# State products as 64x64 blocks on the four quarters of the array, in a new issue order

## The chip, the cores and the metric

The program runs on one core of one Trainium2 chip. The metric is the device time of one execution in microseconds. The kernel before takes 740.38 us, the median of 3 runs (739.6 to 740.51). One further execution was recorded by the hardware profiler; the rows below are of that one.

## The reference

The kernel computes three layers one after the other, all in float32 (4 batches, 8 heads, 576 positions, head size 64; 2304 tokens of width 512):

```python
scores = scale * np.matmul(q, k.transpose(0, 1, 3, 2))
gamma = 1.0 - 2.0 ** (-5.0 - np.arange(H))                    # one decay per head
Dmat = np.where(rel >= 0, gamma[:, None, None] ** rel, 0.0)   # rel = query position - key position
x = np.matmul(scores * Dmat, v)                               # retention; heads side by side: 2304 x 512

h = x @ w_in                                                  # 512 -> 1024
e = np.exp(h - h.max(-1)); sm = e / (e.sum(-1) + 1e-09)
solu = h * sm
ln = (solu - solu.mean(-1)) / np.sqrt(solu.var(-1) + 1e-06) * g_ln
x = ln @ w_out                                                # 1024 -> 512

r = np.maximum(x @ w_in2, 0.0)                                # 512 -> 2048
out = (r * r) @ w_out2                                        # 2048 -> 512
```

The weights of both feed-forward layers arrive as 64-bit floats and are taken apart on the chip.

## The kernel before, in words

The 2304 tokens are 18 tiles of 128. The retention is computed tile by tile in linear form: within a tile scores, mask and values; from tile to tile a running state (the sum of k times v for each head, 64x64), which is started anew at each of the 4 batches.

The order of the whole work is written out by hand in the string `ORDER`: one letter is one step, and a letter's n-th appearance is its n-th tile (or weight job). Each engine executes its share of the steps in that order. A number behind a letter below (S14) is that count, from 0. The letters that matter here:

- `q`, `k`, `v`, `l`: loads of queries (256 tokens, two DMAs), keys, values (128 tokens) and of one half-megabyte weight piece (`raw`), all issued by SyncE's queue. Each issue waits until the one eight before it has landed.
- `D`, `d`: decays of q and k (GpSimd; for the first tile VectorE). `T`, `t`: transposes of q (for two tiles) and k on TensorE, copied out by ScalarE.
- `S` (a_sc): scores of a tile, 8 products of 64 rows, into two banks; VectorE multiplies each bank by the mask.
- `K` (a_kv): the state's own products, 8 of 64x64, copied out by ScalarE into `st`, a 128x128 block for each pair of heads, whose two off-diagonal 64x64 blocks stay zero (two memsets at the start).
- `U` (a_state): state times queries, 4 products with that 128x128 block. It has nothing to do at the first tile of a batch. `V` (a_pv): masked scores times values, 8 products, added into the same bank `x`; ScalarE copies the bank to `x2`.
- `f`, `c`, `h`, `o`: decoding of one weight piece: ScalarE, then VectorE (three operations, L152 to L154) and GpSimd (one), then ScalarE (the high part) and VectorE (the rest: L168 for w_in and the last layer, L170 for w_out). Pieces 0 to 7 are w_in, 8 to 15 w_out, 16 to 47 the last layer's.
- `A`, `B` (m1): the two halves of x @ w_in; VectorE takes the maximum. `E`, `N`, `s`, `P`: softmax and norm on ScalarE and VectorE. `Z` (ln_T): transposes, out by ScalarE and VectorE.
- `m` (m2): a 128x256 piece of ln @ w_out, 24 matmuls over all eight w_out pieces. `3`, `4`: the last layer's two products for 384 tokens. At its end each 128 tokens are copied to an output tile `o` (two buffers) and sent by two DMAs.

All products in these layers are three matmuls (high times high, high times rest, rest times high). Score, state and value products are plain float32, which the profile records as two matmuls each.

PSUM has eight banks: five of them (`r_bank`) go round among q and k transposes, scores, `x`, `Z` and `m`, in the order in which they are asked for; two are for `A`, `B` and `3`; one is for the state `st`.

Of the kernel before, what the change touches and what calls it, by code (L numbers as in the profile page):

```python
# [8 lines left out]
F32 = mybir.dt.float32  # L9
# [3 lines left out]
AF = mybir.ActivationFunctionType  # L13
# [8 lines left out]


ORDER = """
UllkxzqyflkqcfvkhcdtkDldDvfvqThdlkctSvKoSTtfhkoUldqVKckvtVUDdXlhoSkKfdcSvdqVlDfKdTvgUtovcvlAltVSSfXK
DkUTthchUooVVkKSftckhUVfqlolhvfdKkcoSdqTAdvBtEUDVKftNXkcvBTSvlKSdqktDUKldsUhEkcVShNtdqDUkoKfvVdPfVlK
hToctdfAoBSXScTlUtVKDScXfcttUUhofkVsVvKSShUPEhkdNZlVKsZdvABETNlostlotUcVfhohPoKXPASBmmENZmvmcsAZPXfU
BEmSVKlNXvmABUsPcXVENmZmlflKsAZBEmNPlAXsZPFfBZElmhcmNlfAslBhXmEcNsmPAlhXZBElPNlmAZsXBlENsomPAmXBlEmP
oNfcZmXAfXBENsPlcosZhmXABhPmZEmoNZAscllllBhElPNmXmsoomAPBElNsPZmAflBhZEmNsWYmcmPomYmmZlZmhommmmQffcc
3h3ho3fc4fo34h4oc34fhc3ol43fc3hfhf44oco3c434fhhoc3o34fcfh3ohl4fcl34foch3olch43of44ho3c4lf3lhcf3oc4fh  # L30
oc3h3f4o4hfoc343fhocl43hco3fhc43oflh4oc3fc43h4oho433fc44h43o344
"""


# [1 line left out]
def tile_retention_solu_relu2(  # L36
# [19 lines left out]
    nc = tc.nc  # L56
# [4 lines left out]
    P = 128  # L61
# [37 lines left out]
    def r_bank(shape, name):  # L99
        return bank("r", shape, name, 5)  # L100
# [2 lines left out]
    kdecay = at.tile([P, NPAT, H], F32, name="kdecay")  # L103
    masks = at.tile([P, 2, 2, P // 2], F32, name="masks")

    sts = [at.tile([P, KD, P], F32, name=f"st{i}") for i in range(2)]
    ident = const.tile([P, P], F32, name="ident")
    gln = const.tile([P, KF], F32, name="gln")
    mhalf = const.tile([P, 1], F32, name="mhalf")
# [3 lines left out]
    def x_cols(o, n):  # L113
        return x2[o // XG][:, :, o % XG:o % XG + n]
# [50 lines left out]
    def job_lo(j):  # L165
# [3 lines left out]
        else:  # L169
            nc.vector.scalar_tensor_tensor(l, t, g, h.bitcast(F32), ALU.mult, ALU.subtract)  # L170

    def wi_jobs(c):
        w = slice(c * JC, (c + 1) * JC)
        for i in range(KD):
            jobs.append((
                lambda r_, i=i: nc.sync.dma_start(
                    out=r_, in_=w_in[i * P:(i + 1) * P, 2 * c * JC:2 * (c + 1) * JC]),
                lambda x, i=i: (wi_h, wi_l)[x][i][:, w], None))

    def wo_jobs(i):  # L180
# [95 lines left out]
    def a_kv(t):  # L276
        pos = t * P % S
        if pos + P == S:
            return
        fresh = pos == 0 or pos + P > S  # L280
        r0 = S - pos if pos + P > S else 0
        if fresh:
            state["s"] = bank("s", [P, KD * D], "st", 1)
        p_ = state["s"]
        for c in range(KD):
            for e in range(2):
                h = 2 * c + e
                nc.tensor.matmul(p_[D * e:D * (e + 1), c * D:(c + 1) * D], ks[t][r0:P, h], vs[t][r0:P, h],
                                 start=(fresh and c == 0), stop=True, skip_group_check=True)
        st[t] = sts[t % 2]  # L290
        for e in range(2):
            r = slice(D * e, D * (e + 1))
            nc.scalar.activation(st[t][r, :, r], p_[r].rearrange("p (c d) -> p c d", c=KD), AF.Copy)

    res = {}

    def a_state(t):
        pos = t * P % S  # L300
        if not pos:
            return
        p_ = res[t] = r_bank([P, KD, P], "x")
        i = slice(0, min(P, S - pos) // 2)
        for c in range(KD):
            nc.tensor.matmul(p_[:, c].rearrange("p (e i) -> p e i", e=2)[:, :, i], st[t - 1][:, c],
                             qT[t][:, c, :, i], start=(c == 0), stop=False, skip_group_check=True)

    def a_pv(t):
        fresh = t not in res  # L310
        p_ = r_bank([P, KD, P], "x") if fresh else res.pop(t)
        for c in range(KD):
            for e in range(2):
                nc.tensor.matmul(p_[D * e:D * (e + 1), c], vs[t][:, 2 * c + e], sm[t][:, e, c],  # L314
                                 start=(fresh and c == 0), stop=True, skip_group_check=True)
        nc.scalar.activation(x_cols(t * P, P), p_, AF.Copy)


    xhl, hb, ee, lnv, lnT = {}, {}, {}, {}, {}
# [121 lines left out]
    def m4(i):  # L441
# [6 lines left out]
        for s in range(SUB):  # L448
            t = slice(s * P, (s + 1) * P)
            nc.tensor.matmul(acc[b][s], gh[:, t], uh[:, 1], start=(c == 0), stop=False)  # L450
            nc.tensor.matmul(acc[b][s], gh[:, t], ul[:, 1], start=False, stop=False)  # L451
            nc.tensor.matmul(acc[b][s], gl[:, t], uh[:, 1], start=False, stop=(c == KF2 - 1))  # L452
            if c == KF2 - 1:
                o = bw["p"].tile([P, DM], F32, tag="o", name="o", bufs=2)
                nc.scalar.activation(o, acc[b][s], AF.Copy)

                rows = out[b * TB + s * P:b * TB + (s + 1) * P, :].rearrange("(i e) d -> e i d", e=2)
                for e in range(2):
                    nc.sync.dma_start(out=rows[e], in_=o[D * e:D * (e + 1)])

    for c in range(FF // JC):
        wi_jobs(c)
# [5 lines left out]
    with tc.manual_schedule():  # L468
        make_identity(nc, ident)
        nc.gpsimd.memset(mhalf, -0.5)  # L470
        for x in sts:
            nc.gpsimd.memset(x, 0.0)

        def causal_masks():

# [24 lines left out]
        def rest_units():  # L500
# [5 lines left out]
            cols = x2[0].rearrange("p k n -> p (k n)")  # L506
            for j, tag in enumerate("ant"):
                free_cols[tag] = [cols[:, JC * n:JC * (n + 1)] for n in (2 * j, 2 * j + 1)]

        steps = {  # L510
            "q": a_load_q, "k": lambda t: a_load(t, k, ks, "k", 4), "v": lambda t: a_load(t, v, vs, "v", 4),
# [68 lines left out]
```

## Time and profile before

| what | value |
|---|---|
| median of 3 runs | 740.38 us (739.6 to 740.51) |
| the profiled execution | 738.71 us, of which the span from first to last instruction 737.0 us |
| TensorE (PE) busy | 704.6 us, 96% |
| VectorE (DVE) busy | 412.1 us, 56% |
| ScalarE (ACT) busy | 325.8 us, 44% |
| GpSimd (POOL) busy | 144.3 us, 20% |
| TensorE's mean granted clock | 0.992 of full speed |

The span has three stretches. Up to about 120 us the retention runs, with all loads of q, k, v and the first weight pieces; here the other engines are busy too. From there to about 327 us the first feed-forward layer dominates, then the last one. Busy shares are means over all three.

### The profile page before, as it was taken

What the parts mean: (1) busy time and instruction counts of PE and PEld (TensorE: products, weight loads), DVE (VectorE), ACT (ScalarE), POOL (GpSimd) and SP (SyncE); (2) the same over time, 40 slices, a digit from 0 to 9 for tenths busy, and PEclk for the clock granted to TensorE, in tenths of its full rate; (3) what the DMA queues carried; (4) which work ended last, traced back from release to release, by engine and by line L of the source; (5) the groups of instructions that cost most, each with busy time, mean ns of one, the idle gap of its engine ahead of it and who ended that gap; (6) DMA issues with size and microseconds to landing.
All of it is one profiled execution on the core that took longest, in us unless ns stands there. A gap on an engine that the chain in (4) does not pass through costs nothing.

```text
span 737.0 us, 11541 instructions
## 1 busy us (share of the span) xinstructions
PE 704.6 (96%) x4560; PEld 639.7 (87%) x4560; DVE 412.1 (56%) x735; ACT 325.8 (44%) x645; POOL 144.3 (20%) x129
## 2 busy tenths in 40 slices
PE   1999979999999999999999999999999999999996
PEld 1888868999899898998999989989999899998995
DVE  4688897665765885638888887222332232232221
ACT  4576855444642653535565554322322332233222
POOL 3675671121211321102323231000000000000000
PEclk9999998999999999999999999999999999999998
DMA  9999980110000010103233320300100010001001
GB/s 186 217 207 252 206 199 1 44 44 29 29 29 1 30 58 1 30 3 113 90 111 97 105 86 1 87 1 0 26 20 1 0 44 1 0 1 44 1 0 44
DMA packets 64358, 44.90 MB, mean 61 GB/s; under 512 B 40368, under 2 KB 57904, under 8 KB 64304
## 3 DMA queue, kind: packets, MB, share of 16 engines
q1 hardware_dynamic: 64304, 44.16, 25.6%
q8 instruction: 36, 0.59, 0.3%
q14 instruction: 18, 0.15, 0.1%
HBM read 39.44 MB, written 4.72 MB: 60 GB/s over the span
## 4 chain that ended last, share of the span: by engine, by line
PE 87%; DVE 5%; DMA 3%; issue 1%; ACT 1%; SPq 1%; POOL 1%; ACTq 0%; DVEq 0%; POOLq 0%
PE acc L452 9%; PE acc L451 9%; PE m L428 9%; PE m L426 9%; PE m L427 9%; PE acc L450 9%; PE m L398 5%; PE m L400 5%; PE m L399 5%; PE h L334 4%; PE h L336 4%; PE h L335 4%; PE lnT L388 2%; DMA raw<-in_moe_w_in_dram 2%; PE sc L272 1%; PE x L314 1%
## 5 line engine op out<-in xcount | busy, mean ns | idle before, releaser
L436 DVE TENSOR_TENSOR g<-rl 128x384 f32<-128x384 f32 x96 | 59.2, 617 | 190.4 <-ACT rl L435 189.9
L435 ACT ACTIVATE rl<-m 128x384 f32<-128x384 f32 x96 | 46.8, 488 | 194.3 <-PE m L428 194.2
L428 PE MATMUL m<-xh,ul 128*128 128x384 f32 x384 | 129.4, 337 | 0.0
L426 PE MATMUL m<-xh,uh 128*128 128x384 f32 x384 | 129.2, 336 | 0.0
L427 PE MATMUL m<-xl,uh 128*128 128x384 f32 x384 | 128.9, 336 | 0.0
L452 PE MATMUL acc<-uh,gl 128*128 128x512 f32 x288 | 113.9, 395 | 0.5 <-DVE gl L438 0.5
L451 PE MATMUL acc<-ul,gh 128*128 128x512 f32 x288 | 113.6, 394 | 0.0
L450 PE MATMUL acc<-uh,gh 128*128 128x512 f32 x288 | 112.0, 389 | 0.0
L398 PE MATMUL m<-lh,woh 128*128 128x256 f32 x288 | 82.0, 285 | 0.0
L400 PE MATMUL m<-lh,wol 128*128 128x256 f32 x288 | 81.5, 283 | 0.0
L399 PE MATMUL m<-ll,woh 128*128 128x256 f32 x288 | 81.3, 282 | 0.0
L426 PEld LDWEIGHTS m<-xh,uh 128*128 128x128 f32 x384 | 72.2, 188 | 3.8
L427 PEld LDWEIGHTS m<-xl,uh 128*128 128x128 f32 x384 | 72.1, 188 | 3.7
L438 DVE TENSOR_TENSOR gl<-g,gh 128x384 fp32r<-128x384 f32 x96 | 63.8, 665 | 17.1 <-ACT gh L437 5.4
L428 PEld LDWEIGHTS m<-xh,ul 128*128 128x128 f32 x384 | 72.0, 188 | 0.0
L452 PEld LDWEIGHTS acc<-uh,gl 128*128 128x128 f32 x288 | 54.0, 187 | 12.4 <-DVE gl L438 1.0
L437 ACT ACTIVATE gh<-rl 128x384 fp32r<-128x384 f32 x96 | 50.5, 526 | 30.4 <-PE acc L451 14.4
L451 PEld LDWEIGHTS acc<-ul,gh 128*128 128x128 f32 x288 | 54.0, 188 | 9.3
L450 PEld LDWEIGHTS acc<-uh,gh 128*128 128x128 f32 x288 | 54.1, 188 | 8.8
L334 PE MATMUL h<-wih,xh 128*128 128x512 f32 x144 | 57.6, 400 | 0.1
L155 POOL TENSOR_TENSOR x<-x 128x512 int32<-128x512 int32 x24 | 35.1, 1463 | 110.8 <-DVE x L154 93.7
L336 PE MATMUL h<-wih,xl 128*128 128x512 f32 x144 | 56.3, 391 | 0.0
(84 smaller groups left out, 1182.3 us busy)
## 6 DMA issues: line engine op xcount, KB each, us to landing
raw<-in_moe_w_in_dram SPq DMA_DIRECT2D x24, 512.0 KB, 3.9
raw<-in_moe_w_out_dram SPq DMA_DIRECT2D x24, 512.0 KB, 3.3
out_dram<-o SPq DMA_DIRECT2D x36, 128.0 KB, 2.4
k<-in_k_dram SPq DMA_DIRECT2D x16, 256.0 KB, 7.8
q<-in_q_dram SPq DMA_DIRECT2D x16, 256.0 KB, 7.2
v<-in_v_dram SPq DMA_DIRECT2D x16, 256.0 KB, 6.5
q<-in_q_dram SPq DMA_DIRECT2D x4, 128.0 KB, 5.9
k<-in_k_dram SPq DMA_DIRECT2D x4, 128.0 KB, 7.3
```

Of the source, the lines that this page charges most:

```text
L334: nc.tensor.matmul(p_, h_[:, i], wi_h[i][:, cols], start=(i == 0), stop=False)
L336: nc.tensor.matmul(p_, l_[:, i], wi_h[i][:, cols], start=False, stop=(i == KD - 1))
L398: nc.tensor.matmul(p_, wo_h[i][:, w], h_[:, i], start=(i == 0), stop=False)
L399: nc.tensor.matmul(p_, wo_h[i][:, w], l_[:, i], start=False, stop=False)
L400: nc.tensor.matmul(p_, wo_l[i][:, w], h_[:, i], start=False, stop=(i == KF - 1))
L426: nc.tensor.matmul(p_, uh[:, 0, w], xh, start=(j == 0), stop=False)
L427: nc.tensor.matmul(p_, uh[:, 0, w], xl, start=False, stop=False)
L428: nc.tensor.matmul(p_, ul[:, 0, w], xh, start=False, stop=(j == KD - 1))
L438: nc.vector.tensor_tensor(gl, g, gh.bitcast(F32), ALU.subtract)
L450: nc.tensor.matmul(acc[b][s], gh[:, t], uh[:, 1], start=(c == 0), stop=False)
L451: nc.tensor.matmul(acc[b][s], gh[:, t], ul[:, 1], start=False, stop=False)
L452: nc.tensor.matmul(acc[b][s], gl[:, t], uh[:, 1], start=False, stop=(c == KF2 - 1))
```

## The change

Four things change.

1. The state `st` holds only the two diagonal 64x64 blocks of a pair of heads: one copy of 128x256 instead of two of 64x256, and no memsets. `U` has 8 products of 64x64 instead of 4 of 128x128. For an odd pair the results go to the other half of the partitions, so that four products in a row lie on the four quarters of the array. Even pairs go to a bank `x0`, odd ones to `x1`; `V` adds to the same two banks, and two copies of 128x256 bring them out instead of one of 128x512.
2. With odd pairs exchanged, the rows of w_in are exchanged to match: such a piece is loaded by two DMAs of 64 rows.
3. `ORDER` is written anew, with the same letters in the same numbers.
4. Output tiles are six columns of the tokens that are done (`x2[0]`) instead of two buffers. The very last one is copied half by VectorE and half by ScalarE, and its two DMAs are issued from two queues.

```diff
 ORDER = """
-UllkxzqyflkqcfvkhcdtkDldDvfvqThdlkctSvKoSTtfhkoUldqVKckvtVUDdXlhoSkKfdcSvdqVlDfKdTvgUtovcvlAltVSSfXK
...
+llxffklyfkczqlcqfcvdlDhdThkcltDUkfovSKvdTthdVcqvSkktoDflUhKVdcvSUKtVodkqTSXktfcdUlvVKtKShShlDvXhUldV
...
 """
-    sts = [at.tile([P, KD, P], F32, name=f"st{i}") for i in range(2)]
+    sts = [at.tile([P, KD, D], F32, name=f"st{i}") for i in range(2)]
...
+    def wi_load(r_, i, c):
+        w = w_in[i * P:(i + 1) * P, 2 * c * JC:2 * (c + 1) * JC]
+        if i % 2 == 0:
+            nc.sync.dma_start(out=r_, in_=w)
+        else:
+            nc.sync.dma_start(out=r_[:D], in_=w[D:])
+            nc.sync.dma_start(out=r_[D:], in_=w[:D])
...
-        for e in range(2):
-            r = slice(D * e, D * (e + 1))
-            nc.scalar.activation(st[t][r, :, r], p_[r].rearrange("p (c d) -> p c d", c=KD), AF.Copy)
+        nc.scalar.activation(st[t], p_.rearrange("p (c d) -> p c d", c=KD), AF.Copy)
...
+    def halves(c, e):
+        return slice(D * e, D * (e + 1)), slice(D * (e ^ c % 2), D * ((e ^ c % 2) + 1))
+
+    def x_banks():
+        return [r_bank([P, KD // 2, P], f"x{j}") for j in range(2)]

     def a_state(t):
...
-        p_ = res[t] = r_bank([P, KD, P], "x")
+        p_ = res[t] = x_banks()
         i = slice(0, min(P, S - pos) // 2)
         for c in range(KD):
-            nc.tensor.matmul(p_[:, c].rearrange("p (e i) -> p e i", e=2)[:, :, i], st[t - 1][:, c],
-                             qT[t][:, c, :, i], start=(c == 0), stop=False, skip_group_check=True)
+            for e in range(2):
+                r, o = halves(c, e)
+                nc.tensor.matmul(p_[c % 2][o, c // 2].rearrange("p (e i) -> p e i", e=2)[:, :, i], st[t - 1][r, c],
+                                 qT[t][r, c, :, i], start=(c < 2), stop=False, skip_group_check=True)

     def a_pv(t):
...
-                nc.tensor.matmul(p_[D * e:D * (e + 1), c], vs[t][:, 2 * c + e], sm[t][:, e, c],
-                                 start=(fresh and c == 0), stop=True, skip_group_check=True)
-        nc.scalar.activation(x_cols(t * P, P), p_, AF.Copy)
+                o = halves(c, e)[1]
+                nc.tensor.matmul(p_[c % 2][o, c // 2], vs[t][:, 2 * c + e], sm[t][:, e, c],
+                                 start=(fresh and c < 2), stop=True, skip_group_check=True)
+        for j in range(2):
+            nc.scalar.activation(x_cols(t * P, P)[:, j::2], p_[j], AF.Copy)
...
-                o = bw["p"].tile([P, DM], F32, tag="o", name="o", bufs=2)
-                nc.scalar.activation(o, acc[b][s], AF.Copy)
+                last = (b, s) == (NBLK - 1, SUB - 1)
+                o = free_cols["o"].pop(0)
+                free_cols["o"].append(o)
+                if last:
+                    hw = DM // 2
+                    nc.vector.tensor_copy(o[:, hw:], acc[b][s][:, hw:])
+                    nc.scalar.activation(o[:, :hw], acc[b][s][:, :hw], AF.Copy)
+                else:
+                    nc.scalar.activation(o, acc[b][s], AF.Copy)
...
-                    nc.sync.dma_start(out=rows[e], in_=o[D * e:D * (e + 1)])
+                    (nc.scalar if last and e else nc.sync).dma_start(out=rows[e], in_=o[D * e:D * (e + 1)])
...
+            free_cols["o"] = [cols[:, JC * n:JC * (n + 1)] for n in range(6)]
```

How the new order moves instructions is shown at three places. The first is SyncE's queue from its start (`raw` is a weight piece). Before:

```order
L176 DMA raw<-in_moe_w_in_dram 128x1024 x2
L229 DMA k<-in_k_dram 128x8x64
L513 DMA qdecay<-in_tabs_dram 128x144
L221 DMA q<-in_q_dram 64x8x128 x2
L515 DMA kdecay<-in_tabs_dram 128x72
L176 DMA raw<-in_moe_w_in_dram 128x1024
L229 DMA k<-in_k_dram 128x8x64
L221 DMA q<-in_q_dram 64x8x128 x2
```

After:

```order
L175 DMA raw<-in_moe_w_in_dram 128x1024
L178 DMA raw<-in_moe_w_in_dram 64x1024
L179 DMA raw<-in_moe_w_in_dram 64x1024
L536 DMA qdecay<-in_tabs_dram 128x144
L237 DMA k<-in_k_dram 128x8x64
L175 DMA raw<-in_moe_w_in_dram 128x1024
L538 DMA kdecay<-in_tabs_dram 128x72
L237 DMA k<-in_k_dram 128x8x64
L229 DMA q<-in_q_dram 64x8x128 x2
```

A third weight piece now stands ahead of the first queries, and the queries stand behind the second keys. TensorE's first step was the transpose of k (L259 before); it is now that of q, which needs the first queries.

The second place is VectorE late in the retention (L274 before and L282 after are masks of the scores, L152 to L154 the decoding of a weight piece, L170 the rest of a w_out piece). Before, from the decoding of pieces 13 and 14 to the masks of S14 and the first of S15:

```order
L152 TENSOR_SCALAR t<-raw 128x512
L153 SCALAR_TENSOR_TENSOR t<-a,t 128x512
L154 SCALAR_TENSOR_TENSOR t<-raw,t 128x512
L152 TENSOR_SCALAR t<-raw 128x512
L153 SCALAR_TENSOR_TENSOR t<-a,t 128x512
L154 SCALAR_TENSOR_TENSOR t<-raw,t 128x512
L170 SCALAR_TENSOR_TENSOR wol_109<-t,gln,woh_101 128x512
L370 TENSOR_TENSOR r<-r 128x1
L371 SCALAR_TENSOR_TENSOR r<-mv,r 128x1
L274 TENSOR_TENSOR s<-sc_1333,masks 128x4x128
L274 TENSOR_TENSOR s<-sc_1334,masks 128x4x128
L274 TENSOR_TENSOR s<-sc_1346,masks 128x4x128
```

After, from the decoding of piece 15 to the maxima of A3 and B3 (L406 is the rest of a `Z`, wol_113 the last of the eight w_out pieces); the masks of S14 come later:

```order
L152 TENSOR_SCALAR t<-raw 128x512
L153 SCALAR_TENSOR_TENSOR t<-a,t 128x512
L154 SCALAR_TENSOR_TENSOR t<-raw,t 128x512
L406 TENSOR_TENSOR ll<-lnT,lh 128x4x128 x2
L170 SCALAR_TENSOR_TENSOR wol_110<-t,gln,woh_102 128x512
L170 SCALAR_TENSOR_TENSOR wol_111<-t,gln,woh_103 128x512
L170 SCALAR_TENSOR_TENSOR wol_112<-t,gln,woh_104 128x512
L386 TENSOR_TENSOR r<-r 128x1
L387 SCALAR_TENSOR_TENSOR r<-mv,r 128x1
L170 SCALAR_TENSOR_TENSOR wol_113<-t,gln,woh_105 128x512
L356 TENSOR_REDUCE mx<-h 128x1 x2
```

All eight rests of w_out are now made ahead of S14's masks, where before four were made there (the fourth, wol_109, stands in the rows of before). Two norms more, too, stand ahead of them.

The third place is TensorE around the same time. Before, from the end of S15 to the first matmul of A3:

```order
L272 MATMUL sc_1346<-qT,kT 128x128
L272 MATMUL sc_1347<-qT,kT 128x128
L306 MATMUL x<-qT,st_83 128x128 x4
L388 MATMUL lnT<-ident,e 128x128 x8
L314 MATMUL x<-s,v 64x128 x8
L288 MATMUL st<-v,k 64x64 x8
L388 MATMUL lnT<-ident,e 128x128 x8
L334 MATMUL h<-wih_90,xh 128x512
```

After, from the end of S12 to the first score product of S13 (L320 is U, L329 is V, L404 is Z; x_1308 and x_1309 are the two x banks of one tile):

```order
L280 MATMUL sc_1275<-qT,kT 128x128
L404 MATMUL lnT<-ident,e 128x128 x8
L320 MATMUL x_1308<-qT,st_83 64x128 x2
L320 MATMUL x_1309<-qT,st_83 64x128 x2
L320 MATMUL x_1308<-qT,st_83 64x128 x2
L320 MATMUL x_1309<-qT,st_83 64x128 x2
L329 MATMUL x_1308<-s,v 64x128 x2
L329 MATMUL x_1309<-s,v 64x128 x2
L329 MATMUL x_1308<-s,v 64x128 x2
L329 MATMUL x_1309<-s,v 64x128 x2
L296 MATMUL st<-v,k 64x64 x8
L280 MATMUL sc_1345<-qT,kT 128x128
```

Before, one x bank was asked for behind the four banks of S14 and S15. Now two x banks are asked for at each U, and a Z with two banks stands between S12 and U. The first `m`, which needs wol_113, follows behind A3 and B3; before it stood behind B4.

## Rows read from the trace of the kernel before

**Rows 1.** Page: busy us (share, instructions); PE's busy tenths in 40 slices.
```profile
PE 704.6 (96%) x4560; PEld 639.7 (87%) x4560; DVE 412.1 (56%) x735; ACT 325.8 (44%) x645; POOL 144.3 (20%) x129
PE   1999979999999999999999999999999999999996
```

**Rows 2.** Waits of PE, 125 us to the end: us, times, longest.
```profile
PE acc L452 <- DVE gl L438: 0.5, 1, 0.5
```

**Rows 3.** Timeline of DVE and PE at the start: start us, us, instruction, [idle before].
```profile
13.26 0.69 DVE L242 TENSOR_TENSOR k<-k,kdecay 128x512 f32<-128x512 f32 x1 [3.27 <-DMA kdecay<-in_tabs_dram]
...
14.10 1.08 PE L259 MATMUL kTp<-ident,k 128*128 128x128 f32 x4 [14.10 <-DVE k L242]
```

**Rows 4.** Timeline of DVE and PE, 98 to 112 us.
```profile
98.91 1.57 DVE L153 SCALAR_TENSOR_TENSOR t<-a,t 128x512 f32<-128x512 f32 x1
...
103.23 1.57 DVE L153 SCALAR_TENSOR_TENSOR t<-a,t 128x512 f32<-128x512 f32 x1
...
109.19 1.27 DVE L274 TENSOR_TENSOR s<-sc,masks 128x512 f32<-128x512 f32 x2
...
110.01 2.05 PE L306 MATMUL x<-qT,st 128*128 128x128 f32 x8 [5.05 <-DVE s L274]
111.85 1.91 PE L388 MATMUL lnT<-ident,e 128*128 128x128 f32 x8
```

**Rows 5.** Stretches: us; PE, PEld, DVE, ACT, POOL busy (count); PEclk, DMA, GB/s.
```profile
10.00:20.00 10.00, 4.02 (x18) 3.32 (x20) 3.62 (x6) 3.27 (x7) 2.82 (x2) 1.00 1.22 188
...
46.37:109.19 62.82, 55.98 (x653) 49.61 (x652) 55.77 (x81) 44.98 (x89) 45.03 (x36) 0.99 1.02 217
...
110.00:120.00 10.00, 9.99 (x71) 9.01 (x72) 6.94 (x18) 5.78 (x13) 1.56 (x2) 0.76 0.00 0
```

**Rows 6.** The end: chain of waits (start us, us, what), then ACT's last instruction.
```profile
729.96 2.37 DMA out_dram<-o
...
732.43 0.60 ACT L455 ACTIVATE o<-acc 128x512 f32<-128x512 f32 x1 [2.33 <-DMA out_dram<-o]
```

**Rows 7.** Timeline of PE, 93 to 97 us: U, t, V, K, S, t.
```profile
93.00 1.06 PE L306 MATMUL x<-qT,st 128*128 128x128 f32 x8
93.89 0.60 PE L259 MATMUL kTp<-ident,k 128*128 128x128 f32 x4
94.42 1.09 PE L314 MATMUL x<-s,v 128*64 128x128 f32 x16
95.35 0.63 PE L288 MATMUL st<-v,k 128*64 128x64 f32 x16
95.91 1.16 PE L272 MATMUL sc<-qT,kT 64*128 64x128 f32 x16
97.00 0.44 PE L259 MATMUL kTp<-ident,k 128*128 128x128 f32 x2
```

**Rows 8.** Groups by shape, whole span, ACT: busy us, mean ns | idle before.
```profile
L401 ACT ACTIVATE x<-m 128x256 f32<-128x256 f32 x36 | 13.7, 385 | 39.0 <-PE m L400 38.8
L293 ACT ACTIVATE st<-st 64x256 f32<-64x256 f32 x32 | 12.0, 376 | 4.8 <-PE st L288 4.5
```

**Rows 9.** Groups by shape, whole span, DVE.
```profile
L359 DVE BATCH_NORM_STATS2 bs<-e 128x6 f32<-128x512 f32 x36 | 25.0, 694 | 1.2
...
L390 DVE TENSOR_TENSOR ll<-lnT,lh 128x512 fp32r<-128x512 f32 x36 | 23.0, 683 | 9.5 <-ACT lh L389 9.5
...
L168 DVE TENSOR_TENSOR wil<-t,wih 128x512 fp32r<-128x512 f32 x8 | 8.8, 1106 | 0.1
...
L170 DVE SCALAR_TENSOR_TENSOR wol<-t,gln,woh 128x512 fp32r<-128x512 f32 x8 | 5.9, 748 | 2.1 <-ACT woh L162 2.1
```

**Rows 10.** Timeline of PE: T8 begins; the first m0 matmuls of two w_out pieces.
```profile
122.15 1.03 PE L251 MATMUL qTp<-ident,qd 128*128 128x128 f32 x8
...
133.27 0.29 PE L398 MATMUL m<-lh,woh 128*128 128x256 f32 x1
...
133.64 0.28 PE L398 MATMUL m<-lh,woh 128*128 128x256 f32 x1
```

More of the change, by code (lines that the diff above doesn't have):

```diff
@@ L24 @@
 ORDER = """
-UllkxzqyflkqcfvkhcdtkDldDvfvqThdlkctSvKoSTtfhkoUldqVKckvtVUDdXlhoSkKfdcSvdqVlDfKdTvgUtovcvlAltVSSfXK
[L26 to L31, printed above, removed]
+llxffklyfkczqlcqfcvdlDhdThkcltDUkfovSKvdTthdVcqvSkktoDflUhKVdcvSUKtVodkqTSXktfcdUlvVKtKShShlDvXhUldV
+tToUgKffvVocSfqkcklhAqotUlKoDkoVdKSdDBEcldNfTvhAvtqvfcBUvkVkSkclqKhttlThSoUfKXVEsdSvUUDNKVvvVotcPlTo
+kddfSsKUfcdAvkhBPttVcdKSZDlhUEVKoSXfvlNqktchZfohfkooUKshoDVABlmcTEXfmmddtmNSSlstPctTABPUcUXVKVESSNUl
+vXsZVKAZBPEUVNlmKXAlFsZBfPhEXmhhNmAZBsEmmPooNAsPZBmXEmNsAZlBEXPclmNsmlAXBZfXPEmNmlAZsBPENmXABZfEslcP
+XNmmAsBEmPhNZmAmsXfBoZmElNoPmlXsAPcBEfNXZZshmclABPlEhlmNmsoZABWohPElcNhmYYsomPlmZolmmZmmmmmQfclf33hf
+lco3lh4c3oflf4hclo43l3fhc4l3hoc4o34fcfho3hfolc3fhc4434oh3cf4oc3ho43fh4ofc33hcl443ffoh4c43loch3o4hfc4
+of334lcf3hhoc4o3fcf4h3ohf4olc33fh4cofc4ho33h44oc334f4hc4oh4o334
 """
@@ L175, in wi_jobs @@
             jobs.append((
-                lambda r_, i=i: nc.sync.dma_start(
-                    out=r_, in_=w_in[i * P:(i + 1) * P, 2 * c * JC:2 * (c + 1) * JC]),
+                lambda r_, i=i: wi_load(r_, i, c),
                 lambda x, i=i: (wi_h, wi_l)[x][i][:, w], None))
@@ L302, in a_state @@
             return
-        p_ = res[t] = r_bank([P, KD, P], "x")
+        p_ = res[t] = x_banks()
         i = slice(0, min(P, S - pos) // 2)
         for c in range(KD):
-            nc.tensor.matmul(p_[:, c].rearrange("p (e i) -> p e i", e=2)[:, :, i], st[t - 1][:, c],
-                             qT[t][:, c, :, i], start=(c == 0), stop=False, skip_group_check=True)
+            for e in range(2):
+                r, o = halves(c, e)
+                nc.tensor.matmul(p_[c % 2][o, c // 2].rearrange("p (e i) -> p e i", e=2)[:, :, i], st[t - 1][r, c],
+                                 qT[t][r, c, :, i], start=(c < 2), stop=False, skip_group_check=True)
     def a_pv(t):
         fresh = t not in res
-        p_ = r_bank([P, KD, P], "x") if fresh else res.pop(t)
+        p_ = x_banks() if fresh else res.pop(t)
         for c in range(KD):
             for e in range(2):
-                nc.tensor.matmul(p_[D * e:D * (e + 1), c], vs[t][:, 2 * c + e], sm[t][:, e, c],
-                                 start=(fresh and c == 0), stop=True, skip_group_check=True)
-        nc.scalar.activation(x_cols(t * P, P), p_, AF.Copy)
+                o = halves(c, e)[1]
[3 more added lines that the diff above has]
+            nc.scalar.activation(x_cols(t * P, P)[:, j::2], p_[j], AF.Copy)
     xhl, hb, ee, lnv, lnT = {}, {}, {}, {}, {}
@@ L470, in tile_retention_solu_relu2 @@
         nc.gpsimd.memset(mhalf, -0.5)
-        for x in sts:
-            nc.gpsimd.memset(x, 0.0)
         def causal_masks():
```

## The prediction

> **What bounds the kernel now.** I read the page first: TensorE is busy 96% of the span and packed in every slice but the first ones [rows 1]. Next its waits: from 125 us to the end there is one, of 0.5 us [rows 2]. So behind 125 us only less TensorE work, or a shorter tail behind the last matmul, can give time; the large first-layer and last-layer products stay as they are. Then the timeline of the first 125 us, for the places where TensorE sits idle. It starts at 14.10, when the first decayed keys are there, and these waited for a small table behind the first loads [rows 3]. The only other large hole is before U at tile 14: idle 5.05 us, until VectorE had masked S14 at 109.19. VectorE was late because it decoded two weight pieces back to back, with single operations of 1.57 us [rows 4], where one of the same 128x512 elements takes 0.68 elsewhere [rows 9]. After the hole the granted clock of the stretch is 0.76, that is, TensorE had fallen from the upper of its two levels to the lower one for part of it [rows 5]; the Z behind it takes 1.91 for eight matmuls [rows 4]. In that first part three things are close to full: TensorE 56.0 of 62.8 us, VectorE 55.8, and the DMA with 217 GB/s and a share of 1.02 [rows 5]. This is why a gain on TensorE alone need not come out there. Last the chain at the end: the final copy waits 2.33 us for a DMA to free an output buffer, though its matmuls are done [rows 6].
>
> **The tail.** Six output columns instead of two buffers: the last copy no longer waits for a DMA. That returns 2.33 [rows 6], with nothing late behind it, since no other instruction is left. The copy itself, 0.60 [rows 6], becomes two halves side by side; a ScalarE copy of 128x256 takes 0.385 [rows 8], so 0.2. The last two issues go to two queues, so one issue no longer stands behind the other: from the copy's end at 733.03 to the span's end at 737.0 there are 4.0 us, of which the DMA takes 2.37 [rows 6]; of the other 1.6 I take a quarter, 0.4, an estimate. Sum 2.9. Bounds: 2.3 if the halves and the second queue give nothing, 3.1 at best. The copies at the other blocks' ends wait today too, but TensorE does not wait for them [rows 2], so nothing is gained there.
>
> **The state products.** Before, U is eight matmul records in 0.89 us (93.00 to 93.89), 0.111 each. V, with two column halves, does 16 in 0.93, and K 16 in 0.56, S with two row halves 16 in 1.09 [rows 7]: two halves of the array run side by side, one pair in 0.07 to 0.14. New U: 16 records on four quarters. If all four run side by side, four or five rounds of 0.111, 0.45 to 0.56; if only pairs do, 0.89 as now; if none, 1.78. No row shows four. I take 0.50, nearest to what pairs do for both kinds of halves, so 0.39 less for each U, 16 of them, 6.2 in all; bounds 0 and 7.0, or at the very worst minus 14. V keeps its number of products; their order within a pair of heads is exchanged, at nothing. That U is followed by a step of another shape is already so before (K to S, where S takes 1.09).
> On this the trace has one gap: S lets two row halves write, but to two different banks; K lets two column halves write to one bank; no row has two row halves writing one bank, as the even pairs of new U do, each to its own half of the partitions.
> The Trainium skill has a rule against just this: TensorEngine Tiling (Array Packing), section Restrictions and Gotchas, says that different row tiles cannot access the same PSUM bank at once. By that rule U stays near 0.89 and the 6.2 go; this is the third case below. No run here shows it yet.
>
> **ScalarE and GpSimd.** The second copy of x adds at most 18 times 0.385, 6.9; one state copy less takes away 16 times 0.37, 5.9 [rows 8]. ScalarE is busy 45 of 62.8 us in the tight stretch [rows 5], and that idle time hides the 1 us. The two memsets on GpSimd stand ahead of any data and cost nothing. Four more DMA issues for w_in move the same bytes; I put them at nothing, hidden behind landings for which the queue waits anyway; if each held the queue for one landing of 2.37 [rows 6], it would be 9.5, which the case of a slow front below covers.
>
> **The start.** TensorE's first step is now the transpose of q. Ahead of the first queries' end there stand three weight pieces of 512 KB, two keys of 256, both tables (108) and the queries (512), 2668 KB; ahead of the kdecay table before there were 1900. 786 thousand bytes more at 188 GB/s [rows 5] are 4.2 us: TensorE begins at about 18.3 instead of 14.1. In exchange VectorE decodes a third piece while it waits. I do not add these 4.2, because the front's end is set by something else:
>
> **The front.** As the end of the front I take the end of m0, the first piece of ln @ w_out, which needs the last w_out rest (wol_113). When T8 starts before, at 122.15 [rows 10], TensorE has done, against what stands ahead of m0's end in the new order, one T, t, U and V and two S more, but not m0. From rows 7: t 0.53, T with twice its matmuls about 1.0, U 0.89, V 0.93, S 1.09, in all 5.5; m0 is 24 matmuls, three in 0.37 [rows 10], so 3.0. Hence the same work is done before at 122.15 - 5.5 + 3.0 = 119.6. The new order gains in the front what m0 ends earlier than 119.6, its 12 cheaper Us included. Two things bound m0's end from below.
> VectorE: from the masks of S5 (end 46.37) to those of S14 it has 55.8 us of work in 62.8 [rows 5]. The new order has, from the same masks to wol_113, the same nine decodings and eight pairs of masks, and beyond them four w_out rests (3.0), one w_in rest (1.1), a maximum and four norm operations (3.5), two Z rests in four operations (2.7) [rows 9]: 10.3. Short operations on one column come on top and are left out. So wol_113 is done at 46.37 + 55.8 + 10.3 = 112.4 if VectorE never idles, at 119.5 if it idles as much as before.
> DMA: t14 needs the 15th keys. Counting the steps of the order, 16 weight pieces and 15 values stand ahead of them, before 14 and 13, that is 1.57 MB more, at 217 GB/s 7.2 us. Before t14 begins at 97.00 [rows 7], so now at 104.2. Behind it stand a Z (1.0), U 0.5, K 0.56, V 0.93, A3 and B3 (24 matmuls twice as wide as m0's, at most 5.9) and m0, with t14 12.4: 116.6.
> I take 117, a little behind the DMA's bound, in the middle of VectorE's. That is 2.6 gained. The stall of rows 4 is thereby largely exchanged for a later start and for waits on loads and weight rests: most of the 12 Us' gain (4.7) is not seen. The four Us behind m0 stand among packed work and give their 0.39 each, 1.6.
>
> **Sum.** 2.6 + 1.6 + 2.9 = 7.1. Against the profiled execution's own 738.71 this is 731.6. The median of the runs, 740.38, lies 1.67 above that execution, so I forecast 733.3.
>
> **Rivals.**
> Second case, the front packs: VectorE and DMA idle less than before, m0 ends at 112.4. For it: VectorE gets early pieces while it used to wait. Against it: the DMA's 116.6, which would need a higher rate than 217. 7.2 + 1.6 + 2.9 = 11.7, so 728.7.
> Third case, the quarters do not run side by side: U stays at 0.89. The front moves by 0.4 only (the U behind t14), the later Us give nothing: 2.2 + 2.9 = 5.1, so 735.3.
> Fourth case, slower. Its place is VectorE between S6 and wol_113. The five general banks go round; an x pair now takes two, so the U at tile 12 needs the first bank of S12, which VectorE frees only behind two decodings, and A3 a bank freed by a norm. If four more decodings than before run as in rows 4, with each of three operations 0.89 longer (1.57 against 0.68), that is 10.7 us: m0 ends at 127.7, 8.1 behind 119.6, less 1.6 and 2.9, so 744.0. It decides from m0's end at 124.1 on, where front and gains cancel. For it: two decodings did just that in rows 4. Against it: before S14 these two came one behind the other, which the new order does not have there, with m0 needing rests instead.
> Fifth case, no change: m0's end near 124, so 740.4.
>
> **How the numbers follow.** First case 0.50, second 0.20, third 0.15, fifth 0.05, fourth 0.10. A measurement of this kernel can tell 0.2%, 1.5 us, from no change. The first three are faster, 0.85; same 0.05; slower 0.10. The range reaches below the second case's 728.7, since the bounds of U (7.0) and of the tail (3.1) leave another 1 to 2, to 726.5, and above the third to 739.0, where m0 ends at 122.7. The likeliest case's own range is 731 to 736 (m0's end at 114.5 to 119.5).
>
> **What would show it.** The tail: the last copy begins within 0.1 of the last matmul's end. U: 16 records in 0.5 from its start to the next step's; 0.89 would speak for the third case. The start: first TensorE instruction near 18.3. The front: m0's end near 117, with TensorE idle ahead of it in several waits for loads and masks, and no hole of 5 us. From there to the end no wait over 1 us. If m0 ended at 110 or behind 124, or if TensorE waited in the last layer, the prediction would be wrong in its main step.

## The result, and the profile after

The changed kernel takes 730.02 us (median of 4 runs, 729.1 to 730.8), the kernel before beside it 739.99 (4 runs, 738.41 to 740.51): a ratio of 0.9868, interval 0.9847 to 0.9889, faster by 10 us. The forecast was 733.3, in a range of 726.5 to 739.0. The span of the profiled execution went from 737.0 to 728.9.

The page after, for [rows 1]: TensorE is busy 6.7 us less in a span 8.1 shorter.

```profile
PE 697.9 (96%) x4688; PEld 628.9 (86%) x4688; DVE 400.4 (55%) x736; ACT 320.8 (44%) x647; POOL 139.6 (19%) x127
...
PE   0889999999999999999999999999999999999997
```

TensorE's waits over the whole span (us, times, longest), for [rows 2, 3] and the hole of [rows 4]:

```profile
PE qTp L259 <- DVE qd L244: 18.0, 1, 18.0
PE sc L280 <- ACT kT L269: 3.1, 2, 2.0
PE qTp L259 <- POOL qd L244: 2.6, 4, 1.0
PE lnT L404 <- ACT x L332: 0.7, 1, 0.7
PE st L296 <- DMA v<-in_v_dram: 0.6, 1, 0.6
```

It starts at 18.0 instead of 14.1, and then no wait is over 2.0. The hole of 5.05 ahead of U14 is gone, and with it the low clock behind it: the stretches for [rows 5] (columns as there) show a granted clock of 1.00 at 110 to 120 us, where 0.76 stood.

```profile
10.00:20.00 10.00, 1.96 (x10) 1.99 (x11) 6.33 (x10) 2.63 (x5) 3.84 (x3) 1.00 1.21 207
46.37:109.19 62.82, 58.18 (x727) 47.98 (x724) 54.30 (x95) 41.95 (x90) 37.89 (x34) 1.00 1.05 219
...
110.00:120.00 10.00, 10.00 (x73) 9.45 (x72) 9.63 (x15) 4.95 (x11) 4.08 (x4) 1.00 0.51 100
```

PE's timeline, for [rows 7]: U12 (L320), V12 (L329) and K13 (L296). U's sixteen records, now 64x64, stand within 0.60 (99.99 to 100.59), where eight of 128x128 took 0.89.

```profile
99.99 0.67 PE L320 MATMUL x<-qT,st 64*64 64x128 f32 x16
100.59 1.09 PE L329 MATMUL x<-s,v 128*64 128x128 f32 x16
101.61 0.68 PE L296 MATMUL st<-v,k 64*64 64x64 f32 x16
```

The single records of the trace show how: the four of a round start 7 ns apart, the next round 0.11 us after them. The 0.89 is not quite the right thing to compare with, for in [rows 7] a transposition follows U. Where V follows, as here, the eight took 0.99 before (tile 6):

```profile
64.68 1.06 PE L306 MATMUL x<-qT,st 128*128 128x128 f32 x8
65.67 1.09 PE L314 MATMUL x<-s,v 128*64 128x128 f32 x16
```

The first matmul of m0, for [rows 10], and the last w_out rest, which is done at 114.94 while m0 runs:

```profile
113.16 0.29 PE L414 MATMUL m<-lh,woh 128*128 128x256 f32 x1
...
114.20 0.74 DVE L170 SCALAR_TENSOR_TENSOR wol<-t,gln,woh 128x512 fp32r<-128x512 f32 x1
```

The end, for [rows 6]: last matmul, the two half copies, the issues on SyncE's and ScalarE's queues.

```profile
722.98 3.12 SPq L482 DMA_DIRECT2D out_dram<-x  x5
...
723.29 0.39 PE L468 MATMUL acc<-uh,gl 128*128 128x512 f32 x1
723.71 0.42 DVE L475 COPY x<-acc 128x256 f32<-128x256 f32 x1 [2.35 <-PE acc L468]
724.17 0.38 ACT L476 ACTIVATE x<-acc 128x256 f32<-128x256 f32 x1 [0.54 <-DVE x L475]
724.59 0.59 ACTq L482 DMA_DIRECT2D out_dram<-x  x1
```

The copy no longer waits for a DMA, but ScalarE's half waits for VectorE's, and SyncE's five issues of 0.62 each end at 726.10. From the last matmul's start to the span's end it is 5.61 us, where it was 7.24.

### The profile page after: what moved, and what is told of

Its sections match the earlier page's. It is cut to its first block, busy times and chain, and to the rows that moved or that the text cites. A ratio compares the mean times of both kernels' runs of the same rounds, so it can differ in the third digit from the quotient of the medians.

```text
span 728.9 us, 11802 instructions
## 1 busy us (share of the span) xinstructions
PE 697.9 (96%) x4688; PEld 628.9 (86%) x4688; DVE 400.4 (55%) x736; ACT 320.8 (44%) x647; POOL 139.6 (19%) x127
## 4 chain that ended last, share of the span: by engine, by line
PE 90%; DMA 5%; ACT 2%; DVE 1%; issue 1%; SPq 0%; ACTq 0%; DVEq 0%
PE m L444 9%; PE m L442 9%; PE m L443 9%; PE acc L467 9%; PE acc L468 9%; PE acc L466 9%; PE m L416 5%; PE m L414 5%; PE m L415 5%; PE h L350 4%; PE h L351 4%; PE h L352 4%; DMA raw<-in_moe_w_in_dram 3%; PE lnT L404 2%; PE sc L280 2%; DMA raw<-in_moe_w_out_dram 1%
## 5 line engine op out<-in xcount | busy, mean ns | idle before, releaser
L452 DVE TENSOR_TENSOR g<-rl 128x384 f32<-128x384 f32 x96 | 61.9, 645 | 183.7 <-ACT rl L451 182.9
L454 DVE TENSOR_TENSOR gl<-g,gh 128x384 fp32r<-128x384 f32 x96 | 58.8, 613 | 24.7 <-ACT gh L453 12.6
L351 PE MATMUL h<-wil,xh 128*128 128x512 f32 x144 | 56.3, 391 | 0.0
```

Source lines behind the costliest of these rows:

```text
L351: nc.tensor.matmul(p_, h_[:, i], wi_l[i][:, cols], start=False, stop=False)
L452: nc.vector.tensor_tensor(g, rl, rl, ALU.mult)
```

## The experiments

Twelve kernels ran, in three groups, each beside runs of the kernel before (medians 739.94, 739.52, 739.63). The table gives the median and the ratio to before; then, from the profile of one execution, the start of the scores of tile 7 (S7), of m0 and of the last matmul, and the tail, from there to the span's end.

| kernel | median us | ratio, interval | S7 | m0 | last matmul | tail |
|---|---|---|---|---|---|---|
| before | 739.99 | 1 | | | 729.76 | 7.24 |
| changed | 730.02 | 0.9868, 0.9847 to 0.9889 | 61.0 | 113.16 | 723.29 | 5.61 |
| 1 old state products | 728.56 | 0.9854, 0.9835 to 0.9874 | 59.3 | 111.59 | 722.99 | 5.71 |
| 2 before, new tail | 737.55 | 0.9969, 0.9957 to 0.9982 | | | 730.48 | 6.02 |
| 3 old tail | 730.85 | 0.9883, 0.9863 to 0.9903 | 62.4 | 113.63 | 723.95 | 7.05 |
| 4 one DMA per tile | 742.84 | 1.0042, 1.0026 to 1.0058 | 60.7 | 112.42 | 722.55 | 18.85 |
| 5 queries first | 728.24 | 0.985, 0.9833 to 0.9867 | 60.4 | 110.55 | 720.69 | 5.51 |
| 6 fewer loads | 729.15 | 0.9872, 0.9852 to 0.9892 | 59.9 | 111.01 | 721.15 | 5.55 |
| 7 less decoding | 728.26 | 0.985, 0.9833 to 0.9868 | 60.7 | 110.51 | 720.65 | 5.55 |
| 8 last copies on two queues | 729.18 | 0.9861, 0.984 to 0.9883 | 62.2 | 113.06 | 723.19 | 5.11 |
| 9 old products, two banks | 727.98 | 0.9846, 0.983 to 0.9861 | 58.1 | 109.70 | 721.15 | 5.65 |
| 10 both 6 and 7 | 727.66 | 0.9839, 0.982 to 0.9857 | 61.9 | 111.19 | 721.35 | 5.55 |
| 11 both 5 and 8 | 728.62 | 0.9852, 0.983 to 0.9874 | 61.7 | 112.41 | 722.55 | 5.05 |
| 12 as 11, old products | 729.36 | 0.9863, 0.9846 to 0.988 | 59.7 | 111.40 | 722.80 | 5.30 |

Two columns carry much. From m0 to the last matmul it is 610.13 to 610.32 us in all nine kernels with the new products, and 611.40 to 611.45 in the three with the old ones: behind m0 everything is fixed, and only the products count. Ahead of m0 one profile differs from the next: four with the same front (changed, 3, 4, 8) have m0 at 112.42 to 113.63, two others (5, 11) at 110.55 and 112.41. A difference of m0 under 2 us in one profile says nothing.

**1. The old state products.** 128x128 blocks with the two memsets, one bank for x and one copy, w_in in whole loads; new order and tail stay.

```diff
-sts = [at.tile([P, KD, D], F32, ...)]
+sts = [at.tile([P, KD, P], F32, ...)]
-p_ = res[t] = x_banks()      # 8 products of 64x64
+p_ = res[t] = r_bank(...)    # 4 products of 128x128
```

> The changed kernel with its order and its end, but the state products as before: 4 of 128x128 with a zero-padded block, one x bank, one copy. The changed kernel took 730.0. There each U takes 0.60 us from its start to the next step's, against 0.89 before. Theory (VectorE and the loads set the end of m0, so the 12 Us ahead of it are hidden; only the 4 behind it count): 731 to 732, m0 still ends within 1 us of 116.0. Rival (TensorE is the bound of the front, so all 16 Us count): 16 x 0.29 = 4.6, less 18 x 0.05 that V took longer, so 733.5 to 734.5, and m0 ends at 119.

Both missed: 728.56, no later than the changed kernel. The new products, one of the four parts of the change, are worth nothing that can be measured: 0.9868 against 0.9854. In run 1 TensorE is busy 5.6 us longer than in the changed kernel (703.5 against 697.9) in a span of the same length (728.7 against 728.9): with the new products TensorE has less to do and is idle instead. The page's line of this run, and below it that of run 2, which has the same products and the same tail in the old order, with a span of 736.5:

```profile
PE 703.5 (97%) x4560; PEld 638.7 (88%) x4560; DVE 399.0 (55%) x736; ACT 326.8 (45%) x645; POOL 141.9 (19%) x129
PE 706.3 (96%) x4560; PEld 641.2 (87%) x4560; DVE 413.3 (56%) x736; ACT 326.4 (44%) x645; POOL 143.7 (20%) x129
```

**2. The new tail alone**, six columns and the halved copy, in the kernel before.

```diff
-o = bw["p"].tile([P, DM], F32, tag="o", name="o", bufs=2)
+o = free_cols["o"].pop(0)    # and the halved last copy
```

> The kernel before with the changed end alone: six output columns, last copy in two halves, last DMA issued from two queues; order and state as before. Theory from the two traces (from the last matmul's start to the end 7.24 us before, 5.61 changed): 1.6 less than before, 738.4. Rival (the forecast's tail): 2.9 less, 737.1.

737.55: 2.3 us less than before (1.3 to 3.2), which holds both sizes. The tail in the profile went from 7.24 to 6.02.

**3. The old tail in the changed kernel**, the same edit the other way round.

```diff
-o = free_cols["o"].pop(0)    # and the halved last copy
+o = bw["p"].tile([P, DM], F32, tag="o", name="o", bufs=2)
```

> The changed kernel with the end as before (two output buffers, one copy of 128x512, both DMAs from SyncE's queue). Theory: 1.6 more than the changed kernel, 731.6, with the last copy again waiting some 2.3 us for a DMA. Rival (forecast): 2.9 more, 732.9.

730.85; beside 730.02 not told apart by the medians, but the tail is 7.05, as long as before, with the same wait of 2.34 for a buffer. By 2 and 3 the tail gives 1.2 to 1.4 in the profiles.

**4. One copy and one DMA for each output tile.**

```diff
-for e in range(2):
-    (...).dma_start(out=rows[e], in_=o[D * e:D * (e + 1)])
+nc.sync.dma_start(out=rows, in_=o)
```

> The changed kernel with six output columns, each output tile copied by one ScalarE copy and sent by one DMA of 256 KB instead of two of 128 KB. In the changed kernel SyncE's queue issues five output DMAs from 722.98 on, 0.54 to 0.63 us each, and is itself what the last one waits for (issued at 725.47, while its data were ready at 724.55), and the two halves of the last copy ran one after the other. Theory (issue is the bound of the tail): the last issue starts at 724.3, the end 0.7 to 1.0 us earlier, 729.1. Rival (the transfer itself is the bound): a DMA of twice the size lands later by what the issue gains, 729.8 to 730.5.

Both missed, by 13 us. The front is as in the changed kernel (m0 at 112.42); the loss stands behind the last matmul. The stretches of this kernel there (columns as in [rows 5]; no engine is busy):

```profile
725.00:730.00 5.00, 0.00 (x0) 0.00 (x0) 0.00 (x0) 0.00 (x0) 0.00 (x0) 0.64 0.12 45
730.00:735.00 5.00, 0.00 (x0) 0.00 (x0) 0.00 (x0) 0.00 (x0) 0.00 (x0) 0.50 0.13 51
735.00:740.00 5.00, 0.00 (x0) 0.00 (x0) 0.00 (x0) 0.00 (x0) 0.00 (x0) 0.50 0.13 52
```

A DMA share of 0.13 is as much as two of the sixteen engines give, here 51 to 52 GB/s: the last three tiles, 786 thousand bytes, need 15 us. That the DMA's pattern has an outer dimension of two (two interleaved row sets of 64 partitions) fits this; no other pattern was tried, so this reason is not shown.

**5. The first queries ahead of the third weight piece.**

```diff
-llxffklyfkczqlcqfc...
+llxffkqlyfkczlcqfc...
```

> The changed kernel with the first queries' load ahead of the third weight piece on SyncE's queue, nothing else. Theory (the front's end is set by the stream of loads and by VectorE behind it, not by TensorE's start): the first TensorE instruction comes some 2.4 us earlier (512 KB at 207 GB/s), m0 ends within 1 us of the changed kernel's 116.05, the time is the same within 0.7 us. Rival (TensorE's work from its start on sets the front): the start's 2.4 us come through, the time is 2 to 2.5 us shorter.

The first TensorE instruction came at 17.76, not earlier: VectorE decodes three pieces ahead of these queries' decay, and the third now lands behind them. So the edit did not move the start, and tests nothing of it. The 728.24 is lower by 1.8, but the same front in 11 has m0 at 112.41; a gain is not shown. That the start doesn't set the front is shown by other profiles: 8 starts at 15.90 and the changed kernel at 18.04, with m0 at 113.06 and 113.16.

**6. Fewer loads, 7. less decoding, 10. both.**

```diff
+if nm == "v" and 8 <= t <= 14: dst[t] = dst[7]; return       # 6, 10
-nc.vector.scalar_tensor_tensor(tu, w1, 0xC0000000, ...)
+if j >= 16: nc.vector.scalar_tensor_tensor(tu, ...)          # 7, 10
```

> The changed kernel without the loads of the values of tiles 8 to 14 (those of tile 7 are used in their place, so these tiles' results are not the reference's; all other work is the same): 1.84 MB less, 8.5 us of the stream at 217 GB/s. Theory (the loads end last in the front): t14 begins up to 8.5 us earlier than 103.3, m0 ends at 110 to 114, and the time is 2 to 5 us shorter. Rival (VectorE ends last): t14 may begin earlier, but wol_113 and m0 end within 1 us of where they did, and the time is the same within 0.7 us. Second rival (TensorE itself is full): the same as the first rival, with TensorE's waits in the front gone.

> The changed kernel without the third of VectorE's three decoding operations for weight pieces 0 to 15 (the weights' results are not the reference's; loads and all other work are the same): 16 operations of about 0.73 us, of which 9 stand behind the masks of S5, 6.6 us of VectorE's time in the tight stretch. Theory (the loads end last in the front): m0 ends within 1 us of 116.05 and the time is 0 to 0.7 us shorter. Rival (VectorE ends last): m0 ends 2 to 5 us earlier and the time is 2 to 5 us shorter.

> The changed kernel with both of the earlier reliefs of the front together: values of tiles 8 to 14 not loaded, and the third decoding operation left out for pieces 0 to 15 (results are not the reference's). Each alone brought m0's start from 113.1 to 111.0 and 110.5. Theory (loads, VectorE and TensorE are each close to full, and every relief runs into the next of them): they add only in part, m0 begins at 109 to 110, the time is 726 to 727.5. Rival A (they add: two separate limits, TensorE has room): m0 begins at 108.5 or earlier, the time is under 726. Rival B (TensorE's own steps and its order are the floor already with one): m0 begins at 110.3 to 111, the time is the same as with one.

Without 8.5 us of the loads' stream t14 begins at 102.09, where four profiles with them have 102.91 to 104.49; without 6.6 us of VectorE's work at 101.40; without both at 101.93. m0 moves by 2.15, 2.65 and 1.97 against 113.16, little more than one profile differs from another. In the ratio to before neither 6 (0.9872) nor 7 (0.985) is told apart from the changed kernel (0.9868), so that by the time neither theory nor rival of the first two texts is decided. The two reliefs together give no more than one: rival B of the last text, with m0 0.2 behind its range. Why, the stretch from 55 us to 113 us shows, in the same columns: before, changed, and run 10.

```profile
55.00:113.00 58.00, 51.20 (x570) 45.57 (x567) 49.95 (x78) 38.36 (x74) 36.89 (x31) 0.96 0.97 210
```

```profile
55.00:113.00 58.00, 55.77 (x652) 46.14 (x649) 53.53 (x94) 41.24 (x88) 34.00 (x30) 1.00 1.05 213
```

```profile
55.00:113.00 58.00, 57.91 (x679) 48.99 (x678) 49.21 (x91) 41.41 (x89) 34.37 (x30) 1.00 0.87 185
```

TensorE was idle for 6.8 of these 58 us before and is for 2.2 after; with both reliefs it is full, 57.91. That is the floor of this order: behind 55 us it leaves 2 us to be had from loads and VectorE together. Here the cheaper products do show: from S7 to m0 run 10 needs 49.3 us, the three kernels with the old products 51.6 to 52.3.

**8. The last three copies on VectorE, their DMAs on two queues.**

```diff
-nc.scalar.activation(o, acc[b][s], AF.Copy)          # last: two halves
+nc.vector.tensor_copy(o, acc[b][s])                  # last three tiles
-(nc.scalar if last and e else nc.sync).dma_start(...)
+(nc.scalar if end and e else nc.sync).dma_start(...)
```

> The changed kernel with the last 384 tokens' three copies made whole on VectorE (not on ScalarE, and no halves), and of each tile's two DMAs one issued on SyncE's queue and one on ScalarE's. Theory (the tail behind the last matmul is set by the issues, about 0.6 us each, that stand one behind the other on SyncE's queue, and the two halves of the last copy gain nothing since they run one after the other): the last issue begins at the end of the last copy, about 1 us earlier than now, so from the start of the last matmul to the span's end 4.6 us instead of 5.6, and the time is 0.8 to 1.2 us shorter. Rival (the tail is the landing of the last DMA and what the program does at its end): 5.4 to 5.8 us as now, the time the same within 0.3 us.

Half of it came: the tail is 5.11 here, 5.05 and 5.30 in 11 and 12, against 5.51 to 5.71 in the seven kernels with the new order and the new tail as the change has it. The medians can't tell it. The last instructions (three copies in 2.05, three issues on each queue):

```profile
722.26 2.05 DVE L474 COPY x<-acc 128x512 f32<-128x512 f32 x3 [0.99 <-PE acc L468]
...
722.98 1.82 SPq L480 DMA_DIRECT2D out_dram<-x  x3
722.98 2.07 ACTq L480 DMA_DIRECT2D out_dram<-x  x3
723.19 0.39 PE L468 MATMUL acc<-uh,gl 128*128 128x512 f32 x1
```

The copies end at 724.31, and the span 4.0 later, as long as behind the copy of [rows 6]: issue and landing are what is left.

**9. The old products with x in two banks and two copies**, so as to see whether these eat what the new products give.

```diff
-p_ = res[t] = r_bank([P, KD, P], "x")
+p_ = res[t] = x_banks()
```

> The changed kernel with the state as 128x128 blocks as before (as in the run with the old state products), but with x still in two banks and two copies. Theory (of what the new state products give, the front takes the price of the second bank and the second copy, so that the old products with one bank are no later there): m0 begins at 113 or later, against 111.6 with one bank, and at 112.4 to 113.6 in four profiles of the new products; from m0 to the last matmul 611.4, so the time is 1 to 3 us longer than with one bank (728.6). Rival (the second bank costs nothing, the front just doesn't depend on TensorE's products): m0 begins at 111.0 to 112.2, the time is 728 to 729.

The theory fell: m0 at 109.70, the earliest of all and ahead of the rival's range too, and 727.98, no longer than run 1. Neither the second bank nor the second copy shows as a cost. Its stretches, and below them those of the changed kernel:

```profile
3.00:50.00 47.00, 31.43 (x380) 28.05 (x382) 29.95 (x42) 28.28 (x59) 27.72 (x25) 1.00 1.09 233
47.00:55.00 8.00, 8.00 (x85) 7.04 (x84) 6.23 (x9) 6.92 (x16) 3.17 (x3) 1.00 0.85 218
55.00:113.00 58.00, 57.86 (x606) 50.60 (x605) 53.20 (x98) 42.77 (x92) 33.34 (x29) 1.00 0.98 209
```

```profile
3.00:50.00 47.00, 27.88 (x376) 23.21 (x376) 29.10 (x41) 25.22 (x52) 24.58 (x23) 1.00 1.09 206
47.00:55.00 8.00, 5.58 (x87) 4.33 (x82) 3.83 (x6) 4.15 (x9) 5.16 (x4) 1.00 1.14 248
```

With the old products TensorE is full from 47 us on (8.00 of 8 in all three profiles); with the new ones it is idle for 2.4 of the 8 us to 55, and for 2.2 behind. There it waits for the queries of tiles 6 and 7, and GpSimd, which decays them, for their load. In six of the nine profiles with the new products the granted clock is lower as well in these 8 us, 0.63 to 0.80; it is 1.00 in the three with the old products. Run 8 has the lowest:

```profile
47.00:55.00 8.00, 6.04 (x60) 4.74 (x62) 1.46 (x3) 3.17 (x7) 4.25 (x4) 0.63 1.08 237
```

The waits themselves, first in the changed kernel's timeline:

```profile
47.88 2.73 POOL L244 TENSOR_TENSOR qd<-q,qdecay 128x512 f32<-128x512 f32 x2 [1.09 <-DMA q<-in_q_dram]
...
49.21 0.65 PE L259 MATMUL qTp<-ident,qd 128*128 128x128 f32 x4 [1.02 <-POOL qd L244]
...
50.67 0.66 PE L259 MATMUL qTp<-ident,qd 128*128 128x128 f32 x4 [0.80 <-POOL qd L244]
```

and that of run 9, where the same queries are there 3.7 us earlier:

```profile
44.14 2.06 POOL L244 TENSOR_TENSOR qd<-q,qdecay 128x512 f32<-128x512 f32 x2 [0.27 <-DMA q<-in_q_dram]
...
47.21 1.04 PE L259 MATMUL qTp<-ident,qd 128*128 128x128 f32 x8
```

These two profiles are far apart; others are not. GpSimd's same step in run 1, with the old products, and below it in run 4, with the new ones:

```profile
45.03 2.06 POOL L244 TENSOR_TENSOR qd<-q,qdecay 128x512 f32<-128x512 f32 x2
45.61 2.50 POOL L244 TENSOR_TENSOR qd<-q,qdecay 128x512 f32<-128x512 f32 x2 [0.43 <-DMA q<-in_q_dram]
```

Here the queries are only 0.6 us later. In run 1 TensorE comes to them at 48.40 and does not wait; in run 4 it comes to them at 46.71 and then waits 0.80 for their second half and 1.20 for the next values. So the loads need not be much later for the waits to appear: with the cheaper products TensorE reaches them sooner.

From 3 to 50 us the loads run at 222 to 233 GB/s in the three kernels with the old products, and at 206 to 218 in the changed kernel and the eight runs with the new ones. Of the edits that touch the loads only one stands between run 9 and the changed kernel: the odd w_in pieces come in two DMAs of 64 rows, and each of these is one of the eight that SyncE's queue lets fly, with half the bytes. For this speaks that all three kernels with whole loads have the higher rate in the new order; against it that the kernel before, with whole loads in its own order, has 213 (run 2, with the same front, 208), and that four profiles of one front (changed, 3, 4, 8) differ among themselves by 10, more than the 4 that part 218 from 222. The kernel before:

```profile
3.00:50.00 47.00, 32.47 (x367) 28.69 (x369) 30.50 (x41) 25.51 (x50) 25.48 (x23) 1.00 1.17 213
```

New products with whole loads were not tried. That the gain turns into waits is shown; whether the halved loads are really slower, and why, stays open.

**11 and 12. Both 5 and 8, with the new and with the old products**; the edits are those above.

> The changed kernel with the first queries ahead of the third weight piece and the last three copies on VectorE with their DMAs on two queues. Each alone gave 2.6 us at the start of m0 and 0.5 us behind the last matmul in its profile. Theory (they add, being at different ends): the last matmul starts at about 720.6, the span is 725.7, the time 727 to 728. Rival (the 2.6 us of the queries were a chance of one profile): m0 begins at 112.4 to 113.6, the time 729 to 730.

> The same two edits (first queries ahead of the third weight piece, last copies on VectorE with two queues) with the state as 128x128 blocks as before. Theory (the new state products give about nothing in all: 1.3 us behind m0, and as much taken back ahead of it): the time is within 1 us of the same kernel with the new products. Rival (the 12 Us of the front, 0.36 us less each, come through now that the start is better): the kernel with the new products is 3 to 5 us shorter.

728.62 and 729.36, within 1 us of each other, as the theory of run 12 has it. In run 11 the queries' gain was not there again (m0 at 112.41, as the rival has it; the time lies between the two forecasts). No version is shown to beat the changed kernel: all with the new order, but for run 4, lie between 0.9839 and 0.9883, and each of their intervals overlaps the changed kernel's.

## Why the prediction was right, and where it was not

- **The whole.** Faster, by the order and the tail, as forecast. In the profiles it is 8.1 (737.0 to 728.9) for the 7.1 of the sum. The other 2.2 of the 3.3 between 733.3 and 730.02 are the step to the median: I added 1.67, since the profiled execution of before was one of its shorter ones; that of after, 730.58, lies 0.56 above its median.
- **The order** carries nearly all. Run 1 against run 2, the old products and the new tail with and without it: 0.9854 / 0.9969 = 0.988, some 8.5 us, and 7.8 in the profiles (736.5 to 728.7). Two things make up the 7.8. TensorE is idle for 25.2 instead of 30.2 us, 5.0 less. And it is busy for 703.5 instead of 706.3, 2.8 less for the same products: at 110 to 120 us the granted clock is 1.00 in run 1 and 0.76 in run 2, behind the same hole as in [rows 4].
- **The front**: m0's end 116.05 against 117 (115.3 to 116.5 in the four profiles), so 3.55 gained for 2.6. The number came out, the step "DMA: t14 needs the 15th keys" did not: t14, forecast at 104.2 and found at 103.32, stands right behind S13 with no idle time ahead of it, and run 6 with 8.5 us less of the stream has it only 1.2 earlier. In the changed kernel TensorE waits for decayed queries at 47 to 55 us, and behind that its own work is nearly the floor. VectorE, to which I gave 112.4 to 119.5, had wol_113 done at 114.94, in the middle; without 6.6 us of its work (run 7) m0 comes 2.65 earlier.
- **The start**: 18.04 against 18.3, and rightly not added (runs 8 and changed, above).
- **The state products.** U fell to 0.60, not to 0.50 but clearly not 0.89: the four quarters do run side by side, the even pairs' two row halves in one bank as well. The third case fell with that. That the 0.39 less for each U came out is in part luck: the 0.89 was that of a short one, where V follows it was 0.99, so both ends of the difference were put 0.1 too low. By the rule of the Trainium skill, TensorEngine Tiling (Array Packing), section Restrictions and Gotchas, that different row tiles cannot access the same PSUM bank at once, U would have stayed near 0.89; the trace, with 0.60, disagrees where the two write different halves of the partitions. V12 takes 1.02 (100.59 to 101.61) where [rows 7] have 0.93 for a V, but not through the new products: V12 takes 1.02 in run 1 too. Behind m0 they are worth 1.3 (611.40 to 610.13), for 1.6. That most of the gain ahead of m0 would not be seen was right, and too mild: S7 begins at 59.9 to 62.4 with the new products and at 58.1 to 59.7 with the old, and no run shows the new ones to be faster in all.
- **A step in doubt** is the one on the four more DMAs for w_in, put at nothing, "hidden behind landings for which the queue waits anyway": the loads up to 50 us run at 206 to 218 GB/s with them and at 222 to 233 without (new order, one profile each), but profiles of one front differ by as much as 10. If they are the cause, the step fails by about 3 us (an estimate, 6% of 47), within its bound of 9.5; the runs don't settle it.
- **The tail** was mis-sized: 1.63 for 2.9. The wait is gone (2.25), but the halves cost 0.24 instead of giving 0.2, since they ran one after the other (they read one bank and write one tile; which of the two holds ScalarE back was not tried), and the end lies 4.35 behind the copy, 0.38 more than the 3.97 before, since SyncE's last issue stands behind four others.
- **Behind m0** 1.6 was forecast; 2.9 came (6.47 between the last matmuls, less 3.55): 1.3 from U and 0.5 from the one wait of [rows 2]. The other 1.1 is open. It isn't the clock, which was 1.00 before as well from 122.15 on; as the 119.6 from which the 3.55 is counted is an estimate, part of it may belong to the front.

```profile
122.15:729.76 607.61, 606.96 (x3496) 553.67 (x3495) 319.88 (x596) 250.17 (x499) 73.08 (x61) 1.00 0.12 34
```

## What to carry to other kernels

Where TensorE, VectorE and the loads are all nearly full, cheaper products can turn into idle time, as here, and an order that fills the idle time is worth more; look for the stretch in which TensorE becomes full, since that is the floor. A gain that a tight stretch swallows must be looked for as a wait for another engine or a load, here at 47 to 55 us. Two halves of one copy on two engines are only faster if they don't wait for each other; look at the wait before counting on it.

## What was not expected of the hardware

- Sixteen 64x64 matmul records on four quarters take 0.60 us to the next step's start, eight of 128x128 0.99 with V behind them and 0.89 with a transposition (before).
- One DMA of two interleaved sets of 64 rows of 2 KB ran at the share of two of the sixteen DMA engines, 52 GB/s; as two DMAs of 64 rows the same tiles end 13 us earlier (tail 18.85 against 5.61).
- The granted clock, 1.00 in the last 3.5 us of packed work (719 to 722.5 us), was 0.64 on average in the 5 us from 2 us behind the last matmul and 0.50, the lower of its two levels, in the 10 us after that, with TensorE idle throughout (run 4). From 47 to 55 us, where TensorE is idle for 2.0 us in run 8 and 2.4 in the changed kernel, it was 0.63 in the one and 1.00 in the other; why is open.
